# Sliding-window attention beside a gated MLP: more buffers between the steps of a head unit, and divisions and stores placed further behind it

## The chip, the cores and the metric

The kernel runs on one core of one Trainium2 chip. A core has five engines that run side by side, each through a queue of its own in a fixed order: TensorE (PE in the profile; its weight loads are PEld), VectorE (DVE), ScalarE (ACT), GpSimd (POOL) and SyncE (SP), which here issues nearly all DMAs. They meet only through semaphores. The time is device microseconds (us) of one execution, the median of several runs. Three runs of the kernel before took 1860.76, 1861.42 and 1868.03 us: median 1861.42.

## The reference

The block normalises `x` (2048 tokens, 576 wide) and computes two things from it: a causal attention with 32 heads of 18 and a window of 256 keys, and a gated MLP that mixes along the sequence. The result is `x + s * silu(B)`.

```
q, k, v = split((xn @ wqkv), 32 heads of 18)
scores  = q k^T / sqrt(18), only where 0 <= query - key < 256
s       = softmax(scores) v, heads joined, @ wo
z       = gelu(xn @ w_in);  z1 = z[:, :2304];  z2 = layernorm(z[:, 2304:])
g       = w_sp @ z2 + b_sp
B       = (z1 * g) @ w_out
out     = x + s * silu(B)
```

## The kernel before

The program has five stages one after the other, given here by TensorE's work in the trace. Up to 428 us: normalisation, q and k, v, and z2. From 428 to 892 us: the attention's heads, with the product z1 = x·w_z1 filled in between. From 892 to 953 us: the output projection `wo`. From 953 to 1641 us: w_sp·z2 by seven block products per group. From there to the end: the product with w_out.

Only the second stage is touched. It works in 16 units (`UNITS`): four heads for one half of the tokens, first eight units for the first half, then eight for the second. For a unit these steps follow each other:

- `max_item` (L600, L604): scores of 128 queries, whose row maxima VectorE finds; `max_split`, `max_end` and `move` put them, by a transpose and four DMAs, beside the unit's q as extra rows.
- `scores` (L724): the scores again, keys by queries, less the maxima; ScalarE takes the exponential into a tile `pt` of four heads by three blocks of 128 queries (L728); GpSimd cuts the band's edges with one or two masks (L736, L739).
- `pv` (L752): P·V from `pt` into the PSUM tile `ops`. P·V uses all 128 rows of TensorE's array; scores, maxima and z1 use one half of the rows each, `ma` and heads 0 and 2 the first half, `mb` and heads 1 and 3 the second, so that two of them run side by side. In V a column of ones gives the row sums.
- At 512 finished queries ScalarE copies `ops` to a tile `ou` (L767). When a unit's 1024 are there, `finish` sends the sums to a small tile `den` by DMA (L814), VectorE inverts them (L787), they go to memory (L789) and come back spread over 32 rows each as `rp` (L794); GpSimd multiplies `ou` by `rp` in four parts (L798, `divide`), and four DMAs store the parts of four heads (L803, `store`).

z1 is the filling: 18 rows of blocks, each two times 27 matmuls for each half of the array (L671). ScalarE copies each finished bank to a tile `z1o` (L676), and a DMA takes it to memory (L573).

The order of all this is written by a planner in the kernel's own Python. It keeps a clock and times by which each engine would be free, asks at each step whether P·V, scores, a maximum or a z1 matmul is next, and writes the instruction down. `after(ns, fn)` puts a step on a list of due times, and `tick` writes it down once the clock has passed it: loads, stores, the inversion (`INVERT_AT` after `finish`), `rp` (`FETCH_AT` after the inversion), the four divisions and four stores (the eight times of `DIVIDE_AT`). So the numbers set the place of an instruction in its engine's queue, and not the time at which it runs. P·V is held back until two tiles wait, and either nine blocks are together or all of `PTB` tiles `pt` are in use:

```
return n if size >= 9 or len(pts) >= PTB or not score_queue[0] else 0
```

The last unit has no filling behind it but the rest of z1, and `wo` reads what it stores. Its steps stand in `last` and are called from the loop over 16 token blocks in the next stage: `den_load` (L810) ahead of it, `put_last` (L807, L808), `sums`, `divide` and `store` in its first three turns. `wo_load` (L978, L980) reads back stored attention, `wo_split` (L1143 to L1145) makes a high and a low part of it, `wo_half` (L1157) multiplies, and ScalarE copies the result to one of two tiles `so` (L1190), whose DMA (L1192) is issued one turn later.

Of the kernel before, what the change touches and what calls it, by code (L numbers as in the profile page):

```python
# [9 lines left out]
F32 = mybir.dt.float32  # L10
# [6 lines left out]
P = 128  # L17
S = 2048
D = 576
# [12 lines left out]
HS = S // 2  # L32
SLOT = HS + HS + 256
UNITS = [(g, half) for half in range(2) for g in range(8)]
NU = len(UNITS)
# [11 lines left out]
LOAD_STEP = 700  # L47
INVERT_AT = 6500
FETCH_AT = 8500
DIVIDE_AT = (20000, 21200, 22400, 23600, 26500, 27000, 27500, 28000)  # L50
WARM = 54
SPB = 3
PTB = 5


ET = mybir.EngineType
# [3 lines left out]
def f32(ap):  # L60
    return ap.bitcast(F32)
# [3 lines left out]
def kernel(  # L65
# [170 lines left out]
    with ExitStack() as early:  # L236
# [281 lines left out]
        slots = [aa.tile([P, SLOT], F32R, name=f"att{i}", bufs=1) for i in range(3)]  # L518

        with ExitStack() as ph:  # L520
# [33 lines left out]
            waiting = []  # L554
# [3 lines left out]
            def after(ns, fn):  # L558
                waiting.append((clock + ns, fn))
# [7 lines left out]
                return busy[engine] + drain  # L567

            def tick():
                for w in list(waiting):  # L570
                    if w[0] <= clock:
                        waiting.remove(w)
                        w[1]()  # L573
# [85 lines left out]
            def z1_rows(r):  # L659

                for f in range(FH // P):
                    z1_at[r] = f
                    if f not in z1w:
                        z1w[f] = load_z1(f)
                    wh, wl, jobs = z1w[f]
                    while jobs:
                        jobs.pop(0)[0]()
                    for b in range(2):
                        ps = fillp.tile([P, 512], F32, name=("ma", "mb")[r])
                        for n, (w, x_) in enumerate(moving_x(wh, wl, slice(b * 512, (b + 1) * 512), r)):  # L670
                            pe.matmul(ps, w, x_, start=n == 0, stop=n == STEPS - 1)  # L671
                            spend(r, MM + 3)
                            z1_done[r] += 1
                            if n == STEPS - 1:
                                zo = zw.tile([P, 512], F32, name="z1o", bufs=2)
                                act.activation(zo, ps, AF.Copy)  # L676
                                bank_free[r] = use("act", 480, 120) + 100
                                after(bank_free[r] - clock + KEEP_NS,
                                      partial(sp.dma_start, z1_tokens[f * P:(f + 1) * P, b, :, r],
                                              zo.rearrange("p (a q) -> p a q", a=2)))  # L680
                            if f + 1 < FH // P and min(z1_at) == f:
                                if b == 0 and n == 0 and f + 1 not in z1w:
                                    z1w[f + 1] = load_z1(f + 1)
                                if b == 1 and n % 4 == 2 and f + 1 in z1w and z1w[f + 1][2]:
                                    job, engine, ns = z1w[f + 1][2].pop(0)
                                    job()
                                    use(engine, ns)
                            yield
# [13 lines left out]
            vgs, pts, left, o_ps, ous, last, todo, later = {}, {}, {}, {}, {}, [], [], []  # L702
# [39 lines left out]
            def pv(u, kb, qa, qz):  # L742
                g, half = UNITS[u]
                pt = pts[u, kb]
                k0 = 0 if half == 0 else 6
                c = qa // 4
                first = max(4 * c - 2, 0)
                if kb == first:
                    o_ps[c] = ops.tile([P, 512], F32, name="ops")
                hi = min(4 * c + 3, qz)  # L750
                for j in range(4):
                    pe.matmul(o_ps[c][32 * j:32 * j + 32, (qa - 4 * c) * P:(hi - 4 * c + 1) * P],  # L752
                              vgs[u][:, kb - k0, j * VW:j * VW + 32], pt[:, j, (qa - kb) * P:(hi - kb + 1) * P],
                              start=kb == first, stop=kb == 4 * c + 3, skip_group_check=True)
                spend_both((hi - qa + 1) * 218)
                if hi == qz:
                    pts.pop((u, kb))
                else:
                    later.append([0.0, u, kb, hi + 1, qz])
                if kb == 4 * c + 3:  # L760
                    if c % 2 == 0:
                        while parts.get(u - 2):
                            part(u - 2)
                        ous[u] = (ap_.tile([P, HS], F32, name="ou", bufs=2) if u < NU - 1 else
                                  tail()[:, 0:HS])
                    ou = ous[u]
                    act.activation(ou[:, c % 2 * 512:c % 2 * 512 + 512], o_ps.pop(c), AF.Copy)  # L767
                    free_at = use("act", 500, 120)
                    for t in later:
                        t[0] = free_at  # L770
                    if c % 2 == 1:
                        finish(u, ou)

            parts = {}

            def part(u):
                if parts[u]:
                    parts[u].pop(0)()

            def finish(u, ou):  # L780

                g, half = UNITS[u]
                cs = slice(half * HS, half * HS + HS)
                den = aa.tile([P, HS // 32], F32, name="den")
                rp = ap_.tile([P, HS], F32, name="rp", bufs=1) if u < NU - 1 else f32(slots[4][:, 0:HS])
                def invert():
                    dve.reciprocal(den, den)  # L787
                    t = use("dve", 270) - clock + 300
                    after(t + (1500 if u < NU - 2 else 300), lambda: sp.dma_start(r_d[u].rearrange("h (a b) -> (h a) b", b=HS // 32), den))  # L789
                    for i in range(4):  # L790
                        after(t + (FETCH_AT if u < NU - 2 else 4500) + 400 * i, partial(sums, i))

                def sums(i):
                    sp.dma_start(rp[32 * i:32 * i + 32, :], r_d[u][i:i + 1, :].to_broadcast([32, HS]))  # L794

                def divide(a, n=4):
                    hs = slice(a * HS // n, (a + 1) * HS // n)
                    pool.tensor_tensor(ou[:, hs], ou[:, hs], rp[:, hs], ALU.mult)  # L798
                    use("pool", 2900 / n)

                def store(i):
                    h = 4 * g + i
                    sp.dma_start(o_d[h * DH:(h + 1) * DH, cs], ou[32 * i:32 * i + DH, :])  # L803

                if u == NU - 1:
                    def put_last():
                        dve.reciprocal(den, den)  # L807
                        sp.dma_start(r_d[u].rearrange("h (a b) -> (h a) b", b=HS // 32), den)  # L808

                    last.extend([lambda: sp.dma_start(den, ou[DH::32, :]), put_last,  # L810
                                 lambda: [sums(i) for i in range(4)], lambda: [divide(a, 2) for a in range(2)],
                                 lambda: [store(i) for i in range(4)]])
                else:
                    after(busy["act"] - clock + 1000, lambda: sp.dma_start(den, ou[DH::32, :]))  # L814
                    sooner = 10000 if u == NU - 2 else 0
                    after(max(INVERT_AT - sooner, 4500), invert)
                    parts[u] = [partial(divide, a) for a in range(4)] + [partial(store, i) for i in range(4)]
                    for ns in DIVIDE_AT:
                        after(ns - sooner + (3500 if sooner else 0), partial(part, u))

            def sp_combos(stack):

# [26 lines left out]
            with ExitStack() as gate:  # L849
# [66 lines left out]
                zw = open_pool(weights, "zw", bufs=2, side="right")  # L916
# [86 lines left out]
            with ExitStack() as heads:  # L1003
                order.close()
                heads.enter_context(tc.manual_schedule(engines=ENGINES | {ET.Activation, ET.SP}))
                ap_ = open_pool(heads, "attn", bufs=2)
# [61 lines left out]
                while score_queue[0] or score_queue[1] or todo or filling:  # L1068
# [29 lines left out]
                    u, n, j = score_queue[r].pop(0)  # L1098
# [7 lines left out]
                        wo_splits.pop(0)()  # L1106
                    if u == NU - 1 and n % 4 == 0 and n // 4 < 5:
                        if n == 0:
                            while parts.get(u - 2):
                                part(u - 2)  # L1110
                            wors = [tail()[:, HS:HS + D],
                                    ap_.tile([P, HS], F32, name="ou", bufs=2)[:, :D]]
                        if n == 8:
                            wors.append(ap_.tile([P, 10, 89], F32, name="vg").rearrange("p a b -> p (a b)")[:, :D])
                        load_wo(n // 4)
# [92 lines left out]
    with ExitStack() as ph:  # L1208
# [212 lines left out]
        for m, (g, n, s) in enumerate(order_sp):  # L1421
# [26 lines left out]
            if g == 1 and n < 5:  # L1448
                k0, w = 2 * n, 1 if n == 4 else 2
# [238 lines left out]
```

## Time and profile before

| | |
|---|---|
| median of three runs | 1861.42 us |
| the profiled execution | 1859.38 us, its span 1857.3 us |
| TensorE busy in the span | 1823.3 us (98%) |
| VectorE, ScalarE, GpSimd busy | 1138.2, 947.8, 430.7 us |
| attention stage, 428 to 892 us | 464 us, TensorE busy 451.14 |
| `wo` stage, 892 to 953 us | 61 us, TensorE busy 59.65 |
| P·V in the attention stage | 1408 records, 453.1 to 885.5 us |
| last z1 matmul | starts at 891.6 us |

A row of the profile's timeline has the start, the length (of all `xN` that it joins), the engine, the line, the operation, `out<-in` by the program's names, the shape, and in brackets how long the engine sat idle before it and what released it. A row of the view of waits has the waiting engine and line, what it waited for, and the sum in us, the number and the longest. A row of the view by windows has the stretch, its length, the busy time of PE, PEld, DVE, ACT and POOL with the number of instructions, TensorE's granted clock, the DMA engines' busy share and GB/s. TensorE overlaps matmuls, so that a matmul of 512 columns lasts about 0.39 us though the next of its half starts 0.23 us later; busy time therefore says little of how full both halves of the array are.

### The profile page before, as it was taken

To read this page: it belongs to the slowest core of one execution; us is meant where nothing else is said; L and a number is where in the kernel's file an instruction comes from. 1 tells how busy PE (TensorE), PEld (TensorE's weight loads), DVE (VectorE), ACT (ScalarE), POOL (GpSimd) and SP (SyncE) were. 2 spreads that over 40 slices of the span, in tenths; PEclk is the share of its full clock that TensorE was granted. 3 is DMA by queue.
4 is the path that set the end of the run, shared out by engine and by line. 5 is a ranking of instruction groups with operands and counts; after the bars stand their busy time and mean duration, and the time that the engine had idled before them with its cause. 6 is when DMAs were issued, how large, how long until landed. Compare 5 with 4: busy or idle time off the path is not lost.

```text
span 1857.3 us, 38172 instructions
## 1 busy us (share of the span) xinstructions
PE 1823.3 (98%) x14363; PEld 1590.3 (86%) x14363; DVE 1138.2 (61%) x2289; ACT 947.8 (51%) x1758; POOL 430.7 (23%) x507
## 2 busy tenths in 40 slices
PE   8999999999999999999999999999999999999998
PEld 8999999997777777776898878888888888899998
DVE  6321333467766677771246788667876567758876
ACT  5433322225666576667467566465554544444443
POOL 3332333334465455556100000111100000000000
PEclk9999999999999999999999999999999999999999
DMA  8885688887566666754776777789777656786554
GB/s 254 206 229 169 232 278 281 290 258 224 154 194 168 187 174 179 189 161 142 239 266 225 236 239 244 258 293 302 252 262 234 185 183 198 250 266 187 160 159 134
DMA packets 266920, 405.75 MB, mean 218 GB/s; under 512 B 52336, under 2 KB 180592, under 8 KB 266608
## 3 DMA queue, kind: packets, MB, share of 16 engines
q1 hardware_dynamic: 266736, 403.32, 70.4%
q8 instruction: 113, 1.85, 0.4%
q14 instruction: 71, 0.58, 0.1%
HBM read 285.35 MB, written 117.09 MB: 217 GB/s over the span
## 4 chain that ended last, share of the span: by engine, by line
PE 82%; DVE 7%; DMA 5%; SPq 2%; ACT 2%; issue 2%; POOL 0%; DVEq 0%; ACTq 0%; POOLq 0%
PE acc L1431 34%; PE mb L206 11%; PE c L1522 7%; PE ma L671 6%; PE mb L671 5%; PE ma L206 5%; PE ops L752 4%; PE tps L724 3%; PE sp L600 3%; PE wops L1157 2%; SPq L363 1%; DMA st_d<-qkhl 1%; DVE junk L604 1%; DVE spl L116 1%; PE ma L380 0%
## 5 line engine op out<-in xcount | busy, mean ns | idle before, releaser
L1431 PE MATMUL acc<-spl,zh 128*128 128x512 f32 x1008 | 392.6, 390 | 1.1 <-DVE spl L116 0.9
L1431 PE MATMUL acc<-sph,zh 128*128 128x512 f32 x1008 | 392.2, 389 | 0.0
L1431 PE MATMUL acc<-sph,zl 128*128 128x512 f32 x1008 | 392.1, 389 | 0.0
L604 DVE CUSTOM_DVE_ANT_0 junk<-sp,band 128x384 bf16<-128x384 f32 (+1 forms) x512 | 276.4, 540 | 114.9 <-PE sp L600 33.6
L728 ACT ACTIVATE pt<-tps 128x384 f32<-128x384 f32 (+2 forms) x576 | 231.2, 441 | 121.6 <-PE tps L724 78.0
L116 DVE TENSOR_TENSOR spl<-spr,sph 128x1024 fp32r<-128x1024 f32 x168 | 210.2, 1251 | 40.0 <-ACT sph L115 39.3
L671 PE MATMUL mb<-b,z1wh 64*128 64x512 f32 x648 | 225.2, 400 | 2.5 <-ACT z1o L676 2.1
L671 PE MATMUL ma<-b,z1wh 64*128 64x512 f32 x648 | 224.8, 399 | 0.6 <-ACT zt L948 0.4
L1431 PEld LDWEIGHTS acc<-spl,zh 128*128 128x128 f32 x1008 | 189.2, 188 | 41.7 <-DVE spl L116 2.8
L1431 PEld LDWEIGHTS acc<-sph,zh 128*128 128x128 f32 x1008 | 189.3, 188 | 39.3
L1431 PEld LDWEIGHTS acc<-sph,zl 128*128 128x128 f32 x1008 | 189.3, 188 | 39.3
L115 ACT ACTIVATE zh<-b 128x384 fp32r<-128x384 f32 x168 | 87.3, 520 | 211.1 <-PE acc L1431 206.7
L115 ACT ACTIVATE sph<-spr 128x1024 fp32r<-128x1024 f32 x168 | 176.0, 1048 | 14.5 <-DMA spr<-in_w_sp_dram 5.3
L724 PE MATMUL tps<-att 56*128 56x384 f32 (+1 forms) x576 | 177.2, 345 | 2.2 <-ACT pt L728 1.2
L116 DVE TENSOR_TENSOR zl<-b,zh 128x384 fp32r<-128x384 f32 x168 | 99.6, 593 | 124.0 <-ACT zh L115 123.9
L600 PE MATMUL sp<-att 54*128 54x384 f32 (+1 forms) x512 | 161.2, 349 | 2.0 <-DVE mx L604 1.8
L1522 PE MATMUL c<-b,o 128*128 128x288 f32 x1056 | 143.3, 295 | 0.5 <-DVE o L116 0.5
L1522 PEld LDWEIGHTS c<-b,o 128*128 128x128 f32 x1056 | 141.0, 188 | 0.8 <-DVE o L116 0.7
L949 DVE BATCH_NORM_STATS2 st<-zt 128x6 f32<-128x384 f32 x96 | 49.3, 548 | 132.1 <-ACT zt L948 132.0
L671 PE MATMUL ma<-b,z1wl 64*128 64x512 f32 x324 | 128.4, 396 | 0.0
L671 PE MATMUL mb<-b,z1wl 64*128 64x512 f32 x324 | 127.8, 394 | 0.0
L724 PEld LDWEIGHTS tps<-att 56*128 56x128 f32 x576 | 99.7, 184 | 30.5 <-issue 9.5
(219 smaller groups left out, 4189.6 us busy)
## 6 DMA issues: line engine op xcount, KB each, us to landing
spr<-sc_d SPq DMA_DIRECT2D x96, 512.0 KB
spr<-in_w_sp_dram SPq DMA_DIRECT2D x72, 512.0 KB
zr<-z_d SPq DMA_DIRECT2D x144, 192.0 KB
z_d<-zt SPq DMA_DIRECT2D x48, 384.0 KB
z_d<-z1o SPq DMA_DIRECT2D x72, 256.0 KB
z1t<-z_d SPq DMA_DIRECT2D x72, 256.0 KB
y_d<-z1t SPq DMA_DIRECT2D x72, 256.0 KB
a<-in_w_sp_dram SPq DMA_DIRECT2D x64, 256.0 KB
```

The costliest lines, as they stand in the source:

```text
L115: act.activation(hi, src, AF.Copy)
L116: dve.tensor_tensor(lo, src, f32(hi), ALU.subtract)
L206: pe.matmul(banks[h][:, :n], *both[h][i], start=i == 0, stop=i == STEPS - 1)
L600: pe.matmul(ps[:, :w], q_of(u, j)[0:54, i * P:(i + 1) * P], k_of(u, j)[0:54, k0:k0 + w], start=True, stop=True)
L604: dve.tensor_tensor_reduce(out=junk[:, :w], in0=ps[:, :w], in1=band[:, m0:m0 + w], scale=1.0, scalar=-3.0e38, op0=ALU.add, op1=ALU.max, ac ...
L671: pe.matmul(ps, w, x_, start=n == 0, stop=n == STEPS - 1)
L724: pe.matmul(ps[:, :m * P], k_of(u, j)[:, (kb - base) * P:(kb - base + 1) * P], q_of(u, j)[:, (a - lo) * P:(a - lo + m) * P], start=True, s ...
L728: act.activation(pt[:, j, d0:d0 + n * P], ps[:, (qa - a) * P:(qa - a + n) * P], AF.Exp, scale=scale)
L752: pe.matmul(o_ps[c][32 * j:32 * j + 32, (qa - 4 * c) * P:(hi - 4 * c + 1) * P], vgs[u][:, kb - k0, j * VW:j * VW + 32], pt[:, j, (qa - kb) ...
L949: dve.bn_stats(st2[:, s, pc, :], zv)
L1431: pe.matmul(acc[j], z[:, ps], w[:, cs], start=s == i == 0 and n in OPENS, stop=s == 7 and i == 2, skip_group_check=True)
L1522: pe.matmul(banks[key][:, :288], y, w, start=begin and k == n == 0, stop=close and k == 8 and n == 2, skip_group_check=True)
```

## The change

Buffers: six tiles `pt` instead of five (`PTB`, which also enters the planner's rule above), three `ou` instead of two, two `rp` instead of one, three `z1o` instead of two. `ou` is given again only when the unit three back has been stored, and no longer two back; since `rp` has two buffers, `finish` first writes down what is left of the divisions of the unit two back. The due times of divisions and stores are later, by 4 us for the divisions and by 6.5 to 8 us for the stores; for the last unit but one they are moved forward by 10.5 us, where they were by 10 less 3.5. `tick` goes through the due list in order of time.

```
-DIVIDE_AT = (20000, 21200, 22400, 23600, 26500, 27000, 27500, 28000)
+DIVIDE_AT = (24000, 25200, 26400, 27600, 33000, 34000, 35000, 36000)
...
-PTB = 5
+PTB = 6
...
             def tick():
-                for w in list(waiting):
+                for w in sorted(waiting, key=lambda w: w[0]):
                     if w[0] <= clock:
...
-                                zo = zw.tile([P, 512], F32, name="z1o", bufs=2)
+                                zo = zw.tile([P, 512], F32, name="z1o", bufs=3)
...
                     if c % 2 == 0:
-                        while parts.get(u - 2):
-                            part(u - 2)
-                        ous[u] = (ap_.tile([P, HS], F32, name="ou", bufs=2) if u < NU - 1 else
+                        while parts.get(u - 3):
+                            part(u - 3)
+                        ous[u] = (ap_.tile([P, HS], F32, name="ou", bufs=3) if u < NU - 1 else
                                   tail()[:, 0:HS])
...
                 cs = slice(half * HS, half * HS + HS)
+                while len(parts.get(u - 2, ())) > 4:
+                    part(u - 2)
                 den = aa.tile([P, HS // 32], F32, name="den")
-                rp = ap_.tile([P, HS], F32, name="rp", bufs=1) if u < NU - 1 else f32(slots[4][:, 0:HS])
+                rp = ap_.tile([P, HS], F32, name="rp", bufs=2) if u < NU - 1 else f32(slots[4][:, 0:HS])
...
                     for ns in DIVIDE_AT:
-                        after(ns - sooner + (3500 if sooner else 0), partial(part, u))
+                        after(ns - (10500 if sooner else 0), partial(part, u))
...
                         if n == 0:
-                            while parts.get(u - 2):
-                                part(u - 2)
+                            while parts.get(u - 3):
+                                part(u - 3)
                             wors = [tail()[:, HS:HS + D],
-                                    ap_.tile([P, HS], F32, name="ou", bufs=2)[:, :D]]
+                                    ap_.tile([P, HS], F32, name="ou", bufs=3)[:, :D]]
```

No instruction is added or taken away: the stage has 1944 z1 matmuls, 576 scores, 480 maxima (32 more lie ahead of it), 16 transposes and 704 P·V matmuls (1408 records) before and now. Their order is another one nearly from the stage's start on. In the queue of TensorE, P·V stands in 71 separate groups before and in 56 now. Lines after `finish` have numbers higher by two (L798 is L800, L1157 is L1159).

Three places at the stage's end show it. First TensorE's queue around the last P·V, before (`tps` are scores, `ops` is P·V, `ma` and `mb` are z1 in the two halves of the array; 46 more z1 matmuls follow these rows):

```order
L724 MATMUL tps<-att_2228 128x256
L752 MATMUL ops<-pt,vg 32x384 x4
L752 MATMUL ops<-pt,vg 32x256 x4
L671 MATMUL ma<-b_92,z1wh 128x512
L671 MATMUL mb<-b_92,z1wl 128x512
L671 MATMUL ma<-b_95,z1wh 128x512
L671 MATMUL mb<-b_92,z1wh 128x512
L752 MATMUL ops<-pt,vg 32x128 x4
L671 MATMUL ma<-b_92,z1wl 128x512
L671 MATMUL mb<-b_95,z1wh 128x512
```

And the same place now, up to the first matmul of `wo`:

```order
L671 MATMUL ma<-b_97,z1wh 128x512
L671 MATMUL ma<-b_94,z1wl 128x512
L724 MATMUL tps<-att_2227 128x256
L724 MATMUL tps<-att_2228 128x256 x2
L752 MATMUL ops<-pt,vg 32x128 x4
L752 MATMUL ops<-pt,vg 32x256 x4
L752 MATMUL ops<-pt,vg 32x384 x8
L724 MATMUL tps<-att_2227 128x256 x2
L724 MATMUL tps<-att_2228 128x256 x2
L752 MATMUL ops<-pt,vg 32x256 x4
L752 MATMUL ops<-pt,vg 32x128 x4
L1159 MATMUL wops<-att_2229,ohl_14855 128x288 x2
```

Before, 48 matmuls of z1 stood behind the last P·V; now none does, the last z1 matmul of the second half of the array (`mb`) stands 39 rows ahead of `wo`, and the last two groups of P·V stand directly behind scores. Next the queue of SP at the stage's end, before (`att<-o_d` is a `wo_load`, `o_d<-ou` the stores of the last unit but one, `den<-att` the sums of the last unit, `zr` data of the next stage):

```order
L978 DMA att_14354<-o_d 128x4x256
L980 DMA att_14354<-o_d 64x256 x2
L803 DMA o_d<-ou 18x1024 x4
L573 DMA z_d<-z1o 128x2x256 x2
L978 DMA att_2227<-o_d 128x4x256
L980 DMA att_2227<-o_d 64x256 x2
L978 DMA att_2228<-o_d 128x4x256
L980 DMA att_2228<-o_d 64x256 x2
L810 DMA den<-att_14354 128x1x32
L149 DMA zr<-z_d 128x384 x4
L808 DMA r_d<-den 128x32
```

And now:

```order
L980 DMA att_14456<-o_d 128x4x256
L982 DMA att_14456<-o_d 64x256 x2
L796 DMA rp<-r_d 32x1024 x4
L573 DMA z_d<-z1o 128x2x256
L980 DMA att_2227<-o_d 128x4x256
L982 DMA att_2227<-o_d 64x256 x2
L980 DMA att_2228<-o_d 128x4x256
L982 DMA att_2228<-o_d 64x256 x2
L805 DMA o_d<-ou 18x1024 x4
L812 DMA den<-att_14456 128x1x32
L149 DMA zr<-z_d 128x384 x4
L810 DMA r_d<-den 128x32
```

The four stores of the last unit but one moved from ahead of the last two `wo_load` to behind them, directly ahead of the sums of the last unit. Last the end of GpSimd's queue, before (`ou<-ou,rp` are divisions of the last unit but one, `pt<-pt` masks, the last row divides the last unit):

```order
L798 TENSOR_TENSOR ou<-ou,rp 128x256 x2
L736 AFFINE_SELECT pt<-pt 128x4x128
L739 AFFINE_SELECT pt<-pt 128x4x128
L798 TENSOR_TENSOR ou<-ou,rp 128x256 x2
L736 AFFINE_SELECT pt<-pt 128x4x128
L739 AFFINE_SELECT pt<-pt 128x4x128
L736 AFFINE_SELECT pt<-pt 128x4x128 x2
L798 TENSOR_TENSOR att_14354<-att_14354,att_6849 128x512 x2
```

And now:

```order
L739 AFFINE_SELECT pt<-pt 128x4x128
L736 AFFINE_SELECT pt<-pt 128x4x128
L800 TENSOR_TENSOR ou<-ou,rp 128x256 x3
L736 AFFINE_SELECT pt<-pt 128x4x128
L800 TENSOR_TENSOR ou<-ou,rp 128x256
L800 TENSOR_TENSOR att_14456<-att_14456,att_6849 128x512 x2
```

Three of the four divisions of the last unit but one now stand directly ahead of the stage's last mask, where four masks stood behind the last division before.

## The prediction

> **What bounds the kernel now.** I read the view by windows for the stages, the waits of the attention stage, and the timeline of each engine at the stage's end and at its longest stop.
>
> ```profile
> 428.00:892.00 464.00, 451.14 (x4425) 344.39 (x4426) 293.99 (x1041) 303.93 (x742) 243.57 (x355) 1.00 0.64 177
> 892.00:953.00 61.00, 59.65 (x444) 59.19 (x445) 16.38 (x19) 29.51 (x43) 3.61 (x2) 1.00 0.74 241
> ```
>
> Columns: busy time of PE, PEld, DVE, ACT, POOL, granted clock, DMA share, GB/s. TensorE bounds both stages that the change can reach: it is busy 451 of 464 us, and no other engine reaches 350. So time is won or lost only in what TensorE does one after the other. It can be idle little more than 13 us, and yet the stage could be shorter, since two instructions side by side and one alone both count as busy. Its waits:
>
> ```profile
> PEld mb L671 <- ACT z1o L676: 6.9, 16, 1.9
> PEld tps L724 <- ACT pt L728: 6.9, 21, 1.3
> PEld ops L752 <- ACT pt L728: 4.1, 12, 0.4
> PEld ops L752 <- POOL ou L798: 1.6, 4, 1.0
> PE ops L752 <- POOL ou L798: 0.8, 1, 0.8
> POOL ou L798 <- DMA rp<-r_d: 9.9, 5, 3.0
> SPq L803 <- POOL ou L798: 20.1, 6, 8.1
> ACT z1o L676 <- DMA z_d<-z1o: 1.6, 1, 1.6
> ```
>
> The reader is to see that ScalarE's copies and exponentials hold TensorE longer than anything that the new buffers free, and that divisions wait for `rp` (9.9 us) and stores for divisions (20.1 us) without TensorE feeling much of it.
>
> **1. The order of TensorE.** Between two groups of P·V (or transposes) the halves of the array run side by side, and such a stretch lasts as long as its fuller half.
>
> ```profile
> 889.22 0.40 PE L671 MATMUL ma<-b,z1wh 64*128 64x512 f32 x1
> 889.45 0.39 PE L671 MATMUL ma<-b,z1wl 64*128 64x512 f32 x1
> 883.13 0.38 PE L724 MATMUL tps<-att 56*128 56x256 f32 x1
> 883.29 0.39 PE L671 MATMUL mb<-b,z1wh 64*128 64x512 f32 x1
> 883.62 1.28 PE L752 MATMUL ops<-pt,vg 128*32 128x384 f32 x16
> 884.83 0.49 PE L671 MATMUL ma<-b,z1wh 64*128 64x512 f32 x1
> 885.16 0.39 PE L671 MATMUL ma<-b,z1wh 64*128 64x512 f32 x1
> 885.49 0.43 PE L752 MATMUL ops<-pt,vg 128*32 128x128 f32 x8
> 885.85 0.49 PE L671 MATMUL ma<-b,z1wl 64*128 64x512 f32 x1
> ```
>
> In one half, 512 columns follow 512 columns after 0.23 us. I take 0.232, and for 384 and 256 columns three quarters and a half of it. Added over the stage's stretches in the two orders, the fuller half is 317.5 us before and 320.3 us now. The 25 matmuls of `ma` behind the last P·V are 5.8 us of the former. Up to the last P·V it is 311.7 us before and 320.3 now: **+8.6 us**. Nothing hides this, since z1 was itself the cover: it is used up earlier, and scores then run beside an empty half.
>
> **2. Fewer groups of P·V.** Five blocks of 128 queries take 1.21 us (883.62 to 884.83), one block 0.36 (885.49 to 885.85): 0.2125 each and 0.147 for the group. To this come 0.10 us ahead of it (883.29 and 0.232 is 883.52, P·V starts at 883.62) and 0.10 behind (884.83 to 885.16 is 0.33 where 0.232 would do): 0.35 us for a group. 71 groups become 56 with the same 360 blocks: 15 × 0.35 = **−5.2 us**, all of it on TensorE's path.
>
> **3. The last P·V without cover.** The last two groups stand directly behind scores.
>
> ```profile
> 883.81 0.27 ACT L728 ACTIVATE pt<-tps 128x128 f32<-128x128 f32 x1
> 884.21 0.63 POOL L736 TENSOR_SCALAR_AFFINE_SELECT pt<-pt 128x512 f32<-128x512 f32 x1 [1.31 <-ACT pt L728]
> 885.99 0.60 ACT L767 ACTIVATE att<-ops 128x512 f32<-128x512 f32 x1 [1.91 <-PE ops L752]
> 886.48 1.26 ACT L1143 ACTIVATE ohl<-att 128x1280 fp32r<-128x1280 f32 x1
> 887.78 1.23 DVE L1144 TENSOR_TENSOR ohl<-att,ohl 128x1024 fp32r<-128x1024 f32 x1 [9.24 <-ACT ohl L1143]
> 891.87 8.39 PE L1157 MATMUL wops<-att,ohl 128*128 128x288 f32 x61
> ```
>
> From the last score (883.13) to the mask's end (884.84) are 1.7 us, of which four scores cover 0.2. With z1 this was covered; alone it is 1.5 us. Twice is **+3.0 us**; once, if the group ahead has its tiles early, is the lower end, and 4.5 the upper, if scores wait for exponentials as well. The last P·V ends at 885.85 before: T. `wo` needs ScalarE's high part, ready 1.9 us after T (887.74), and VectorE's low part at T + 3.2 (889.01), after two products that take 0.54. So `wo` now starts as if at T + 2.65; before, z1 ran until 891.87 and covered all of it. What that costs is decided by step 6.
>
> **4. Third `z1o`.** TensorE's longest stop in this stage:
>
> ```profile
> 633.32 0.38 SPq L573 DMA_DIRECT2D z_d<-z1o  x1
> 639.34 0.40 PE L671 MATMUL ma<-b,z1wl 64*128 64x512 f32 x1
> 640.63 0.60 ACT L676 ACTIVATE z1o<-mb 128x512 f32<-128x512 f32 x1 [1.60 <-DMA z_d<-z1o]
> 641.28 0.49 PE L671 MATMUL mb<-b,z1wh 64*128 64x512 f32 x1 [1.54 <-ACT z1o L676]
> 642.54 0.79 PE L671 MATMUL ma<-b,z1wh 64*128 64x512 f32 x1
> 642.00:644.00 2.00, 2.00 (x14) 1.74 (x13) 0.98 (x4) 2.00 (x5) 1.00 (x2) 0.55 0.64 187
> 644.00:646.00 2.00, 2.00 (x15) 1.95 (x12) 0.93 (x3) 1.10 (x4) 1.19 (x2) 0.60 1.01 150
> ```
>
> A copy waits for the store issued at 633.32, still under way seven us later, and all of TensorE's queue waits behind it: 639.34 to 641.28, 1.94 us, of which 0.2 is the matmul. A third tile takes this away. What follows goes with it: the granted clock falls to 0.55 and 0.60 for two windows of 2 us, (0.45 + 0.40) × 2 = 1.7 us lost. With the stop's 1.7 it is 3.4, and nothing if another wait takes the place; I take **−3.4 us**, as both were seen once and have one cause.
>
> **5. Divisions later, second `rp`, third `ou`.** P·V waited for masks behind a division that waited for `rp`: 0.8 us of TensorE's own idle time up to 2.4 with its weight loads. Four us more leave room for `rp` (longest wait 3.0): **−1.5 us**. The 20.1 us of SP's waits for divisions go as well; behind them stand z1's stores and loads, priced in step 4 where TensorE felt it. The sixth `pt` adds no instruction; its worth is steps 1 to 3. The sorted due list moves rows that are counted there.
>
> **6. The last unit's sums.** The sum so far puts the last P·V at 8.6 − 5.2 + 3.0 − 3.4 − 1.5 = +1.5 us. What ends `wo` is not TensorE but this chain:
>
> ```profile
> 884.41 0.41 SPq L978 DMA_DIRECT2D att<-o_d  x1
> 886.18 0.53 SPq L978 DMA_DIRECT2D att<-o_d  x1
> 888.00 0.62 SPq L810 DMA_DIRECT2D den<-att  x1
> 901.69 3.61 POOL L798 TENSOR_TENSOR att<-att,att 128x512 f32<-128x512 f32 x2 [16.85 <-DMA att<-r_d]
> 905.32 1.37 SPq L803 DMA_DIRECT2D o_d<-att  x4
> 913.54 0.65 ACT L1190 ACTIVATE so<-wops 128x576 f32<-128x576 f32 x1 [8.22 <-DMA s_d<-so]
> 915.40 0.78 PE L1157 MATMUL wops<-att,ohl 128*128 128x288 f32 x4 [0.87 <-ACT ohl L1143]
> ```
>
> The sums leave at 888.00, GpSimd divides at 901.69, the stores go at 905.32, and behind them in SP's queue stand the stores of `so`. ScalarE waits 8.22 us for one of these, the high part of the fourth operand stands behind it, and TensorE waits at 915.40, T + 29.55, for that. Now `wo` would be there at T + 2.65 + 22.7 (six turns of 3.78, 891.87 to 914.5) = T + 25.3, so the chain decides, and the end moves with T and with the place of `den`. Ahead of it now stand two `wo_load` of 1.8 us (884.41 to 886.18) and four stores of 1.37 together, from the last scores on (T − 2.2, with exponential, mask and P·V behind them): T − 2.2 + 3.55 + 1.37 = T + 2.7, against T + 2.15 before: **+0.5 us**; at most +1.4 if the loads start as late as before (884.41 is T − 1.4). The 4.7 us that TensorE now waits in turn six cost nothing more, unless the clock falls again: 0 to 1.7, I take half, **+0.85**.
>
> By the rule in the Trainium skill, TensorE: Matmul & The Clock Gate, Part 1, the rate is halved after a free-running window of about 3.4 us in which the engine had little to do. The stop of 1.94 us and the two windows behind it agree, and by that rule a wait of 4.7 us would nearly always cost the whole 1.7, and the sum would be 0.85 us more.
>
> **The sum.** 1.5 + 0.5 + 0.85 = **+2.85 us** on the profiled execution (1859.38). The median of the runs stands 2.04 us above that; I add to it: 1864.3. What follows `wo` is unchanged work on a busy TensorE and passes a delay on.
>
> **Rivals.** For them one group of the page, 441 ns for an exponential:
>
> ```profile
> L728 ACT ACTIVATE pt<-tps 128x384 f32<-128x384 f32 (+2 forms) x576 | 231.2, 441 | 121.6 <-PE tps L724 78.0
> ```
>
> (a) *Faster: the waits on ScalarE go too.* More tiles let every queue run ahead, so the planner's order meets fewer late copies. For it: 6.9 + 6.9 + 4.1 us in the rows above, less 1.9 counted, is 16. Against it: one bank for each half of z1 and two for scores stay as they are, and these waits are for banks. If 9 of the 16 go, −6.2: 1855. It decides the sign from 2.9 us on, and half a per cent (9.3 us, about what a measurement can tell from no change) from 12. (b) *Slower: the stage's end is worse.* Sixteen scores and three groups of P·V stand behind the last `mb`, and three divisions ahead of the last mask. If the three divisions (3.61 us for two of 512 columns is 0.9 for one of 256, so 2.7) hold up the last mask, and the scores go at the pace of an exponential (0.44 us) instead of their own 0.15, 16 × 0.29 = 4.6 us, it is 7.3 more, +10: 1872. For it: no z1 is left. Against: `ma` has 19 matmuls there. (c) *The chain is hidden*: `den` leaves early or lands fast; then `wo` runs from T + 2.65 without the stop of 1.35 us at turn six: 1.5 + 885.85 + 2.65 − 891.87 − 1.35 = −3.2 us: 1858. Against it: each of its links stands in one queue in order. (d) That the buffers are not used is excluded by the 56 groups.
>
> **How the numbers follow.** The sum 0.45; (a) 0.22; (b) 0.25; (c) 0.08. The sum's own range, with the lower and upper ends of its terms, is 8.6 − 5.2 + 1.5 − 3.4 − 2.4 = −0.9 to 8.6 − 5.2 + 4.5 − 0.8 + 1.4 + 1.7 = +10.2: 1860 to 1872. (a) and (b) widen it to 1855 and 1874. Faster by over 0.5% (below 1852) takes three quarters of (a)'s 16 us: 0.07. Slower by over 0.5% (above 1870.7) is most of (b) and the upper end of the sum: 0.25. Within: 0.68.
>
> **What would show it.** In the new profile: no stop of ScalarE at `z1o` for its store and no low clock near 640 us (4); GpSimd's divisions without a wait for `rp` (5); the last P·V about 887, no z1 behind it, and two stops of TensorE ahead of the last groups (1, 3); a stop of TensorE of 4 to 5 us in turn six of `wo`, with ScalarE waiting for `so` (6). The prediction is wrong if the last P·V stands ahead of 884 or behind 892, or if `wo` runs through.

## The result, and the profile after

The changed kernel takes 1888.98 us (median of five runs, 1885.83 to 1894.26) against 1861.42 before: 1.0148 times as long, 95% interval 1.0130 to 1.0165. It is slower by 27.6 us, where 2.9 and no measurable change were forecast. The profiled execution took 1885.83 us with a span of 1883.8.

First the view by windows of the kernel after, in the stretches used before:

```profile
428.00:892.00 464.00, 440.68 (x4267) 341.82 (x4271) 287.93 (x1035) 291.64 (x710) 233.48 (x341) 0.99 0.64 166
892.00:953.00 61.00, 54.15 (x408) 46.77 (x404) 12.82 (x18) 30.18 (x54) 11.46 (x16) 0.94 0.72 226
```

In the same 464 us TensorE is busy 10.5 us less and gets 158 fewer instructions done. Then the stage's end, in TensorE's timeline of the kernel after:

```profile
909.50 0.55 PE L724 MATMUL tps<-att 56*128 56x256 f32 x2 [0.42 <-ACT pt L728]
909.98 0.64 PE L752 MATMUL ops<-pt,vg 128*32 128x256 f32 x8
911.19 0.43 PE L752 MATMUL ops<-pt,vg 128*32 128x128 f32 x8 [0.57 <-POOL pt L736]
913.54 0.79 PE L1159 MATMUL wops<-att,ohl 128*128 128x288 f32 x4 [1.93 <-ACT ohl L1145]
```

The last P·V starts at 911.19 where it started at 885.49: all but about 1 us of the loss is in the attention stage. From that P·V to the end of `wo` it is 68.5 us (67.8 before), and from there to the span's end 904.0 (903.9 before). TensorE's stops in the stage, counted as steps of over 0.56 us from start to start, are 29 with 27.7 us above a normal step of 0.23; before they were 16 with 13.2. The rows of the view of waits that carry them, after:

```profile
PE ops L752 <- ACT ou L767: 8.7, 10, 1.2
PEld ops L752 <- POOL pt L736: 6.8, 8, 1.2
PEld sp L600 <- DVE mx L604: 6.2, 13, 2.0
PEld ops L752 <- POOL pt L739: 5.7, 9, 1.6
PE tps L724 <- DMA att<-mhl: 3.6, 2, 2.1
PEld mb L671 <- ACT z1o L676: 2.2, 8, 0.5
POOL ou L800 <- DMA rp<-r_d: 1.1, 1, 1.1
POOL ou L800 <- DMA att<-st_d: 16.9, 4, 11.2
DVE den L789 <- DMA den<-ou: 9.3, 5, 3.1
```

And the rows of before that answer to the first three and are not yet shown (the fourth has none there):

```profile
PE ops L752 <- ACT ou L767: 2.0, 2, 1.1
PEld ops L752 <- POOL pt L736: 0.4, 2, 0.2
PEld sp L600 <- DVE mx L604: 6.3, 15, 0.6
```

What the buffers were for has come in part. Copies no longer wait for the store of `z1o`, and P·V no longer waits for a division. The divisions themselves still wait: 1.1 us are put down to `rp` and 16.9 to loads of head data, which a division does not read. It reads `ou` and `rp`, and in the run below where it does not read `rp` none of these waits is left, so `rp` holds it up for 18.0 us, where 15.8 in all stood ahead of divisions before. And P·V now waits ten times for ScalarE's copy of the sums before it, and for masks, and a score waits 2 us for a maximum. Two places show how. TensorE, below it ScalarE, and last a group that is not joined, in the kernel after:

```profile
620.32 0.86 PE L752 MATMUL ops<-pt,vg 128*32 128x256 f32 x16
621.99 1.50 PE L752 MATMUL ops<-pt,vg 128*32 128x384 f32 x16 [0.81 <-ACT ou L767]
...
621.25 0.60 ACT L767 ACTIVATE ou<-ops 128x512 f32<-128x512 f32 x1 [0.34 <-PE ops L752]
...
633.16 0.86 PE L752 MATMUL ops<-pt,vg 128*32 128x256 f32 x16
633.94 0.38 PE L724 MATMUL tps<-att 56*128 56x256 f32 x1
```

Here a group of P·V is *joined*: the last tiles of one accumulator and the first of the next stand side by side, and `ops` has one PSUM bank. So the copy out stands in the middle of the group, and its second half starts 1.67 us behind the first, where what follows the same 16 matmuls at 633.16 starts after 0.78. Nothing else stands between in TensorE's queue. In the kernel before 4 of 71 groups are joined, in the changed one 14 of 56. Beyond 0.2125 us a block and 0.147 a group, groups last 5.5 us in sum before and 16.8 after. In four of the 14 the view puts the wait down to a mask. At the first of them, in the queues of GpSimd, ScalarE and TensorE:

```profile
591.54 0.64 POOL L739 TENSOR_SCALAR_AFFINE_SELECT pt<-pt 128x512 f32<-128x512 f32 x1
592.23 0.60 ACT L767 ACTIVATE ou<-ops 128x512 f32<-128x512 f32 x1 [1.40 <-PE ops L752]
592.93 0.85 PE L752 MATMUL ops<-pt,vg 128*32 128x384 f32 x8 [0.77 <-POOL pt L739]
```

The mask ends at 592.18 and the copy at 592.83, so here too the copy ends last. In two of the other three it does as well, and in the last (743 us) the two end within 0.1 us of each other.

The other place, in the queues of SP, VectorE and TensorE of the kernel after:

```profile
652.90 0.62 SPq L816 DMA_DIRECT2D den<-ou  x1
653.64 1.60 SPq L550 DMA_DIRECT2D att<-st_d  x2
658.51 0.35 DVE L789 RECIPROCAL den<-den 128x32 f32<-128x32 f32 x1 [3.07 <-DMA den<-ou]
659.34 0.44 PE L600 MATMUL sp<-att 54*128 54x384 f32 x1 [1.81 <-DVE mx L604]
```

The gather of sums (16 KB) is issued among loads of head data, and the inversion runs 5.6 us later. In all units but the last where VectorE waited for this gather, it had the sums 2.7 to 5.8 us after the issue in the kernel before, and 5.3 to 7.6 us in the one after. The inversion stands ahead of the maxima in VectorE's queue, so these wait 3.07 us and TensorE 1.81. The clock falls behind some of these stops: after, the granted clock is low inside the stage for 10.2 us (3.4 before) and twice in `wo`. The low clock behind 443 us is not the new order's alone: a later run in the order of before ("No wait for sums, in the kernel before") has 3.4 us of it there too, behind the same wait for the maxima's DMA.

```profile
444.00:446.00 2.00, 2.00 (x11) 1.29 (x10) 1.13 (x4) 1.99 (x3) 0.00 (x0) 0.50 0.92 247
680.00:682.00 2.00, 2.00 (x13) 2.00 (x13) 0.85 (x3) 1.01 (x4) 1.95 (x3) 0.50 0.78 254
```

Put together for the last P·V: fuller half +8.6, fewer groups −5.2, stops +14.5, half of 6.8 us more of low clock +3.4: 21.3 of the 25.7 us. The other 4.4 are not found; waits too short to count as stops, or errors of the worked-out terms, would be the place to look.

### The profile page after: what moved, and what is told of

Same layout as the page of the kernel before. It is cut to its first block, busy times and chain, and to the rows that moved or that the text cites. A ratio compares the mean times of both kernels' runs of the same rounds, so it can differ in the third digit from the quotient of the medians.

```text
span 1883.8 us, 38150 instructions
## 1 busy us (share of the span) xinstructions
PE 1831.5 (97%) x14363; PEld 1589.9 (84%) x14363; DVE 1135.1 (60%) x2289; ACT 950.0 (50%) x1758; POOL 430.7 (23%) x507
## 4 chain that ended last, share of the span: by engine, by line
PE 80%; DMA 7%; DVE 7%; SPq 2%; ACT 2%; issue 2%; POOL 0%; DVEq 0%; ACTq 0%; POOLq 0%
PE acc L1433 34%; PE mb L206 11%; PE c L1524 7%; PE ma L671 6%; PE ma L206 5%; PE mb L671 5%; PE ops L752 4%; PE tps L724 3%; PE sp L600 2%; PE wops L1159 2%; SPq L363 1%; DMA st_d<-qkhl 1%; DVE junk L604 1%; DMA den<-ou 1%; DVE spl L116 1%
## 5 line engine op out<-in xcount | busy, mean ns | idle before, releaser
L724 PEld LDWEIGHTS tps<-att 56*128 56x128 f32 x576 | 101.2, 186 | 40.0 <-issue 17.8
```

Source lines behind the costliest of these rows:

```text
L724: pe.matmul(ps[:, :m * P], k_of(u, j)[:, (kb - base) * P:(kb - base + 1) * P], q_of(u, j)[:, (a - lo) * P:(a - lo + m) * P], start=True, s ...
```

## The experiments

Four theories stood against each other. A: joined groups. B: what the prediction had, z1 that is used up, a fuller half and an uncovered end. C: the later divisions and stores. D, formed after the first four runs: DMAs that come late for an order of instructions that does not wait for them, above all the gather of sums. Ratios are to the kernel before in the same session (medians 1862.4 to 1863.0), with their 95% intervals.

**Buffers alone.** The kernel before, its order unchanged, with the memory of the change:

```
-    bufs=PTB / z1o bufs=2 / ou bufs=2 / rp bufs=1
+    bufs=PTB + 1 / z1o bufs=3 / ou bufs=3 / rp bufs=2
```

> The kernel before with the memory of the change (pt 6, ou 3, rp 2, z1o 3) and the planner's old rules, so that every engine's order is that of before. Theory A (joined groups: with six tiles in the planner's rule a group of P.V joins the last tiles of one bank with the first of the next and stops in the middle for ScalarE's copy): no joined group is added, so no loss; z1o's stop near 640 us and the low clock behind it go, 1856 to 1860. Theory B (z1 runs out early, the fuller half of the array): order as before, so the same 1856 to 1860. Theory C (the later divisions and stores, and what they do to GpSimd and the DMA queue): as before too. If the new places of the buffers in memory cost by themselves, it is slower than 1865.

Measured 1859.97 us, 0.9987 [0.9974, 0.9999]. Memory itself costs nothing; the loss is in the order. The stop for the store of `z1o` is gone, but in the profiled execution one of 1.87 us for a maximum stands at 613.6, with 3.4 us of low clock behind it, and the stops sum to 13.1 us (13.2 before). So where the 2 us come from is not shown.

**Six tiles alone.** The kernel before with one number changed:

```
-PTB = 5
+PTB = 6
```

> The kernel before with PTB = 6 alone. Its order has 14 joined groups (4 before, 14 in the change), the fuller half adds up to 318.7 us and no z1 stands behind the last P.V. Theory A: some 10 stops of 1.03 us more than before, most of the change's loss: 1878 to 1890. Theory B: the fuller half costs 7 us and the uncovered end 3, groups save 5: about 1866. Theory C: no later divisions, so no loss: 1855 to 1862.

Measured 1900.94, 1.0207 [1.0183, 1.0230]: worse than the whole change, with 14 joined groups too. Masks stand behind divisions that wait for the one `rp`, and copies wait for the store of `z1o`:

```profile
PEld ops L752 <- POOL pt L739: 15.1, 14, 5.6
ACT z1o L676 <- DMA z_d<-z1o: 8.5, 2, 4.9
POOL ou L798 <- DMA rp<-r_d: 7.5, 5, 3.8
```

The other parts of the change thus win back 12 us of what six tiles cost, and C as the cause of the loss falls.

**All but the sixth tile.** The changed kernel with

```
-PTB = 6
+PTB = 5
```

> The change with PTB = 5 alone put back: later divisions and stores, three ou, two rp, three z1o. Its order has 67 groups and none joined, fuller half 315.4 us, 28 z1 matmuls behind the last P.V. Theory A: four stops fewer than before, four groups fewer, z1o's stop gone: 1850 to 1858. Theory B: about 2 us less than before: 1857 to 1860. Theory C: the later divisions carry the loss: 1875 to 1890.

Measured 1871.19, 1.0047 [1.0028, 1.0065]. The sixth tile costs 17.8 us, which A and B can both explain. But there is no gain over before, although nothing is joined here and the other buffers are in use. VectorE and TensorE of this run show why:

```profile
622.32 0.35 DVE L789 RECIPROCAL den<-den 128x32 f32<-128x32 f32 x1 [5.47 <-DMA den<-ou]
623.14 0.69 PE L600 MATMUL sp<-att 54*128 54x384 f32 x1 [3.46 <-DVE mx L604]
```

Three such stops make 9.0 us above a normal step, and the low clock in the stage sums to 23.9 us. From this came D.

**Joined groups broken.** The changed kernel, its planner ending a group where the next tile opens a new bank:

```
-                    for _ in range(n):
+                    for i in range(n):
+                        t = todo[0]
+                        if i and t[2] == max(t[3] // 4 * 4 - 2, 0):
+                            t[0] = max(t[0], busy["act"] + 120)
+                            break
                         pv(*todo.pop(0)[1:])
```

> The change, with P.V's group ended where the next tile opens a new bank: 64 groups, none joined, fuller half 324.1 us, no z1 behind the last P.V. Theory A: the 14 stops of 1.03 us go, eight more groups cost 0.35 us each, the fuller half 3.8 us: 1889 - 14.4 + 2.8 + 3.8 = 1881, and the stops in P.V are gone from the trace. Theory B: only the fuller half counts, 1889 + 4 to 1893 or more. Theory C: unchanged, 1887 to 1891.

Measured 1891.01, 1.0149 [1.0126, 1.0171]: no gain. The stops inside joined groups are gone, but the rule makes another order (64 groups, fuller half 324.1 us), and this meets other late loads. ScalarE in this run:

```profile
563.12 0.49 ACT L728 ACTIVATE pt<-tps 128x384 f32<-128x384 f32 x1 [0.23 <-PE tps L724]
568.00 0.52 ACT L686 ACTIVATE z1wh<-z1raw 128x384 fp32r<-128x384 f32 x1 [4.39 <-DMA z1raw<-in_w_z_dram]
```

The low clock rose to 27.3 us. An edit to the planner's rule is no test of the cost it removes; the next runs keep the order and change one cost.

**A shorter copy.** The order of the changed kernel; the copy at L767 takes 64 columns from PSUM, and the other 448 from a tile in SBUF, so that a joined group waits less (those 448 columns of the attention are left out):

```
-    act.activation(ou[:, ...:... + 512], o_ps.pop(c), AF.Copy)
+    act.activation(ou[:, ...:... + 64], o_ps.pop(c)[:, 0:64], AF.Copy)
+    act.activation(ou[:, ... + 64:... + 512], f32(xt6[0])[:, 0:448], AF.Copy)
```

> The change in its own order, but ScalarE's copy of P.V frees the bank sooner: it copies 64 of 512 columns, and a second instruction fills the other 448 from x in SBUF, so those columns of the attention are left out. Theory A (stops inside joined groups of P.V): each of the 14 stops ends some 0.4 us sooner, 5 to 6 us: about 1883, and the stops inside P.V are near 0.7 us in the trace where they were 1.08. Theory B (too little z1 in the right half, uncovered end): 1888 to 1890. Theory D (the new order meets DMAs that land late, and engines wait for them in their fixed order): 1888 to 1890.

```profile
619.61 0.86 PE L752 MATMUL ops<-pt,vg 128*32 128x256 f32 x16
620.90 1.50 PE L752 MATMUL ops<-pt,vg 128*32 128x384 f32 x16 [0.43 <-ACT ou L767]
```

The group of 620.32 above now takes 1.29 us to its second half in place of 1.67. The run is 1883.38, 1.0134 [1.0095, 1.0173]: 5.6 us under the median of the change, though the two intervals overlap. In the trace 13 of the 14 places are shorter by some 0.4 us, the four put down to masks among them: from the last matmul of one accumulator to the first of the next, the 14 take 11.6 us in sum, 16.2 in the changed kernel. More than half of the stop stays. In the profiled execution the last P·V is only 1.2 us earlier, with the clock low for 6.8 us more ahead of it.

**No wait for sums.** Again the changed order; inversion and division read data that is there, so VectorE and GpSimd wait for no gather (the division by the sums is left out):

```
-                    dve.reciprocal(den, den)
+                    dve.reciprocal(inv, mv2.rearrange("p a b -> p (a b)"))
...
-                    pool.tensor_tensor(ou[:, hs], ou[:, hs], rp[:, hs], ALU.mult)
+                    pool.tensor_tensor(ou[:, hs], ou[:, hs], (rp if u == NU - 1 else ou)[:, hs], ALU.mult)
```

> The change in its own order, with two waits for DMAs taken away by other data: for all units but the last VectorE inverts a tile that lies ready instead of the unit's sums, and GpSimd multiplies the output by itself instead of by the spread sums; all DMAs stay. So the division by the sums is left out. Theory D: VectorE's 9.3 us and GpSimd's 18 us of waiting ahead of these go, and with them TensorE's stops for maxima and masks (2.4 and 4.6 us) and a low clock: 1879 to 1884. Theory A and B: 1887 to 1890.

Measured 1881.84, 1.0125 [1.0094, 1.0156]: 7.1 us less than the change. The last P·V starts at 905.7. Its interval, too, overlaps that of the change, so for each of these two the run of both together decides, below.

**The same with five tiles.** The edit just shown and `PTB = 5`.

> The same two waits taken away from the change with PTB = 5 (1871 us, 17 us of VectorE's waiting, three stops of TensorE of 9 us for maxima, four low clocks in the stage). Theory D: these go, 9 us and some of the 8.5 us of low clock: 1855 to 1862. If the waits were only where they show, and something else held the queue: 1869 to 1872.

Measured 1853.96, 0.9952 [0.9934, 0.9969]: 17.2 us less than all but the sixth tile. There the waits for sums, with the low clock behind them, are the whole loss and more; 8 stops with 6.5 us above a normal step remain.

**Break and buffers, on the kernel before.** The planner's rule of the fourth run and the buffers of the first, with five tiles and the old due times.

> The kernel before with the change's memory (as in the first of these runs, 1860 us) and a group of P.V ended where the next tile opens a new bank: 70 groups, none joined, the fuller half 309.4 us up to the last P.V (311.7 before), 16 z1 matmuls behind it. Theory A and B: four stops of 0.85 us and 2.3 us less: about 1854. Theory D: it is a new order of everything, with loads, sums and maxima at other places, and meets late DMAs anew: 1862 to 1880, with VectorE waiting more than 7 us ahead of its inversions or ScalarE for z1's weights.

Measured 1866.25, 1.0022 [1.0005, 1.0040], where A wanted a gain. No group is joined; TensorE waits for maxima behind the inversion instead:

```profile
DVE den L787 <- DMA den<-ou: 13.2, 8, 2.5
PE sp L600 <- DVE mx L604: 4.1, 5, 1.6
```

**Both causes taken away.** The edits of the fifth and the sixth run in one kernel.

> The change in its own order with both causes eased at once: the short copy (448 of 512 columns of the attention left out) and the two waits for sums taken away (the division by the sums left out). If A and D are separate causes, 5.6 and 7.1 us add up: about 1876, and what remains over the kernel before, some 14 us, is its order itself: the fuller half of the array, the end without z1, the waits for maxima and transposes. If they are one cause seen twice: 1880 to 1883.

Measured 1874.78, 1.0065 [1.0045, 1.0084]: 14.2 under the change. The interval lies clear of the change's and of those of the two runs with one edit each, so each edit gains something on top of the other, and both causes are real. Whether the gains simply add is less sure: by medians the two apart give 12.7, but these are of different sessions, and by the ratios to before they give 2.6 and 4.3 against 15.4 together.

**No wait for sums, in the kernel before.** The edit of the sixth run.

> The control: the kernel before in its own order, with the two waits for sums taken away in the same way (division left out). If late sums cost the change because its order puts them badly, before gains little, since VectorE waits 4 us there and no stop of TensorE follows from it: 1857 to 1862. If any order gains 7 us by it, the difference between the two kernels isn't from these waits: 1853 to 1856.

Measured 1858.36, 0.9974 [0.9963, 0.9985]: a gain of 4.6 us where the changed kernel gained 7.1, so these waits explain only some 2.5 of the 27.6 us between the two kernels, and that difference is within the noise. And with the waits for sums gone in all three, the orders give 1858.4 (before), 1854.0 (all but the sixth tile), 1881.8 (six tiles) and 1874.8 (six tiles, the copy shortened too). What the sixth tile costs is in its order.

**Five tiles, inversion later.** All but the sixth tile, with the inversion and its DMA written 3500 ns later for all units but the last two, so that maxima stand ahead of it:

```
+                late = 3500 if u < NU - 2 else 0
-                    dve.reciprocal(den, den)
+                    after(late, lambda: dve.reciprocal(den, den))
...
-                    after(t + (1500 ...
+                    after(t + late + (1500 ...
```

> A correct kernel: the change with PTB = 5, and VectorE's inversion (with the DMA behind it) written down 3.5 us later than the planner's entry; the orders of TensorE and ScalarE are the same as with PTB = 5 alone (1871 us), only the 14 inversions stand further back in VectorE's queue. Theory D: VectorE no longer waits 17 us for sums, TensorE's three stops of 9 us and the low clocks behind them go: 1854 to 1859, below the kernel before. If VectorE's place isn't what counts: 1868 to 1872.

Measured 1855.74, 0.9963 [0.9949, 0.9977]: faster than before and after, and 15.5 us less than without the shift, with TensorE's and ScalarE's queues word for word the same. Its window and its one wait for the gather:

```profile
428.00:892.00 464.00, 458.17 (x4479) 356.13 (x4477) 292.96 (x1042) 302.56 (x742) 247.15 (x357) 1.00 0.68 181
DVE den L790 <- DMA den<-ou: 0.6, 1, 0.6
```

The last P·V starts at 874.3 and the clock is never low from 17 to 1846 us. This settles D for five tiles.

**z1 held back.** For B: the changed kernel keeps the last 25 z1 matmuls of each half until the last P·V, as cover for the end.

```
-    if filling and bank_free[r] <= clock and fill(r):
+    if (filling and bank_free[r] <= clock
+            and (z1_done[r] < total - 25 or not (score_queue[0] or score_queue[1] or todo)) and fill(r)):
```

> The change with the last 25 z1 matmuls of each half held back until the last P.V stands: as many groups and joined groups as the change, the fuller half 314.6 us up to the last P.V (320.3) and 50 z1 matmuls behind it. Theory B, and the chain from the last P.V through the last unit's sums that ends the output projection: the last P.V is 5 us earlier, the projection starts from z1's end and the stop in its sixth turn shrinks: 1882 to 1886. If the missing z1 at the end isn't what counts (TensorE then idles in the last unit instead): 1887 to 1891.

Measured 1893.18, 1.0166 [1.0142, 1.0189]. The end is covered, but the last unit starves instead:

```profile
892.04 2.29 PE L752 MATMUL ops<-pt,vg 128*32 128x128 f32 x24 [0.82 <-issue]
...
901.35 1.07 PE L724 MATMUL tps<-att 56*128 56x384 f32 x2 [0.26 <-ACT pt L728]
...
892.00:906.00 14.00, 12.65 (x64) 6.05 (x64) 3.30 (x5) 7.85 (x17) 3.76 (x7) 0.52 0.62 180
```

Scores run at the pace of exponentials and the clock is halved for 14 us. This too is an edit to the planner's rule, which makes another order, so it is no test of what the end cost. For that there are the rows of the changed kernel: 0.7 us more behind the last P·V, and some 1.5 us of waits just ahead of it.

## Why the prediction was wrong

The forecast was 1864.3, with 1855 to 1874 as its range. It was 24.7 us short, and its own mark for wrong (last P·V behind 892) was passed by 19 us. By its steps:

- **Step 2 is the one that failed.** It took fewer groups as −5.2 us, "all of it on TensorE's path". The groups are fewer because tiles of two accumulators stand in one group, and with one bank that group stops in its middle for a copy. Groups lost 11.3 us more than before (10.5 without the very last one, which waits for its mask), so the step is worth +6.1 where −5.2 was forecast. The rule quoted in front of it (nine blocks or all of `PTB`) and the one bank were both there to read, and so was one row of before, P·V waiting 1.1 us for `ou` L767.
- **The sum had no term for waits that a new order makes.** It went through the waits of before and let each shrink or stay. Nearly every row of the stage is in another place, and the run without the sixth tile shows what that does even where no group is joined: 17 us in waits for sums and the clock behind them.
- **Step 1** (+8.6): the six-tile order, with both causes eased, stays 16 us behind that of before without waits for sums. That has room for it, but no run measured it alone.
- **Step 3** (+3.0): at the end TensorE waits 0.42 and 0.57 us in the rows above and 0.48 once more: 1.5 us, the lower end.
- **Step 4** (−3.4): the wait went as said. "Nothing if another wait takes the place" came for the clock: 10.2 us low instead of 3.4.
- **Step 5** (−1.5): TensorE's waits for masks behind a division went as said, but not since `rp` came in time: the divisions wait for it at least as long as before. The 4.6 us of stops that the view puts down to masks are four of the joined groups of step 2.
- **Step 6** came out nearly as worked out. The sums leave at 914.26, T + 2.7 as forecast, ScalarE waits for `so`, TensorE stops in turn six, and the clock falls:

```profile
914.26 0.80 SPq L812 DMA_DIRECT2D den<-att  x1
938.41 0.65 ACT L1192 ACTIVATE so<-wops 128x576 f32<-128x576 f32 x1 [8.66 <-DMA s_d<-so]
940.28 0.78 PE L1159 MATMUL wops<-att,ohl 128*128 128x288 f32 x4 [2.08 <-ACT ohl L1145]
941.54 4.72 PE L1159 MATMUL wops<-att,ohl 128*128 128x288 f32 x22 [0.48 <-DVE ohl L1146]
```

 The stop is 2.08 us and not 4.7; the low clock from 914.2 on (3.4 us at 0.50) had already made the turns some 1.7 us late, and the rest of the difference was not followed up. In sum +0.7 where +1.35 was forecast.

Rival (b) priced the slower side at 1872 and put it in the wrong place: the three divisions ahead of the last mask end at 909.94, and the mask waits 0.56 us for its exponential. Rival (a) had it the wrong way round: more tiles let the planner fill a group from two accumulators that share one bank.

Open: the 16 us between 1874.8 and 1858.4. In the traces of these two runs the last P·V is 14.0 us apart. Of this +8.6 and −5.2 are worked out from the orders. The stops differ by 5.2 us (26 with 17.8, 15 with 12.6), some 4 of them in joined groups. The low clock ahead of that P·V differs by 3.4 us, which is 1.7. Together that is 10.3, and the rest is not found. No run tested these terms apart, and whether six tiles gain with two banks for `ops` was not tried.

## What to carry to other kernels

A number that sets a planner's threshold is a change of order first and a buffer second: count in the new order where a group crosses a resource that exists once, before pricing what the buffer frees. In a fixed order a small DMA's result must be read late enough for its worst landing, since a waiting instruction holds up all that stand behind it; in the five-tile order the place of the inversion, moved for 14 units, was worth 15.5 us, more than all the buffers. And to test a suspected wait, keep the order and change its cost; a planner that is asked to avoid it gives a new order with waits of its own.

## What the runs showed of the hardware

Where VectorE waited for it, a gather of 16 KB was read from 2.0 to 8.6 us after its issue. The earliest is 866.1 to 868.1 in the run without the sixth tile, the latest 774.14 to 782.69 in the run with z1 held back, among loads of head data.

In the changed kernel, stops of 1.45, 1.93 and 2.12 us of TensorE were each followed by 3.4 or 6.8 us at a granted clock of 0.50, and those of about 1 us inside joined groups and the one of 1.81 at 659.34 were not. The run with z1 held back had 14 us at 0.52 with no idle time over 0.82 us; TensorE had P·V, a few z1 matmuls and scores there, one or two at a time between waits of about 0.26 us.

By the Trainium skill, TensorE: Matmul & The Clock Gate, Part 1, the rate is halved after an idle window of about 3.4 us, and the windows run freely. The pieces of 3.4 us agree. That stops of 1.45 to 2.12 us, shorter than a window, were followed by one does not follow from the rule as stated, and here the measurement decides. A stop of 1.81 us that cost nothing beside one of 1.45 that did would fit if it matters how a stop lies to the window, which no run tested. The run with z1 held back shows that the clock can fall with no long stop at all; what counted there as too little work is not shown.
